# Attention, a rotation block and a feed-forward block on one core: a third score buffer for the first batch, joined first scores, chunks of 512 tokens, and 1/sum applied after P times V

## The chip, the core and the metric

One core of one Trainium2 chip runs the whole program in one launch. The metric is the device time in microseconds (us): the median of three runs of the kernel before is 902.61 us (902.42 to 905.83). The engines are PE (TensorE, matrix products; PEld is its weight load, which overlaps), DVE (VectorE), ACT (ScalarE), POOL (GpSimd) and SP (SyncE, which here only issues DMAs). A bank is one of the eight accumulators of PSUM, 128 partitions by 512 fp32 numbers.

## What is computed

Three blocks follow each other, for a batch of 4 with 576 tokens and a width of 512 (8 heads of 64).

```python
# attention, blocks of 64 tokens, each sees itself and the blocks before it
scores = 1/sqrt(64) * q @ k^T;  scores = where(block_i >= block_j, scores, -1e9)
attn = exp(scores - max(scores));  attn = attn / (sum(attn) + 1e-9);  x = attn @ v
# rotation block
theta = x @ w_theta
y = w_tok_r @ (x * cos(theta)) + w_tok_i @ (x * sin(theta))
u = x + y;  x = u + relu(u @ w_ch)
# low-rank token mixing (rank 32) and feed-forward of width 2048
u = x + (x^T @ U @ V)^T
out = u + relu(u @ w_ch1) @ w_ch2
```

## The kernel before

**A recorder and a planner.** The code does not issue instructions as it runs. `Line` records each one with a due time (`at_time`, `spread`) and a price (`price`, line 275). `run` (line 339) then walks through a list schedule: each engine takes, of what is ready and for which a buffer is free, the entry that is due first. The order so found is written out engine by engine and kept. All recorded instructions therefore carry the one line number L1162 in the profile, and are told apart by the names of their tiles.

**Attention.** The four batches have four pairs of heads each; `gp` counts the 16 pairs. Of a pair, `prep` (636) loads q, k and v and scales q. `smax(gp, t)` (650) forms the scores of token tile t = 0 to 4 for both heads in PSUM: for t = 2 to 4 each tile has a buffer of two banks of its own (tag `ss`, two buffers in all), while tiles 0 and 1 share one, as two separately issued steps. It overwrites the masked corner (a memset on DVE), takes the negated maximum `nm` (DVE), and ACT writes `P = exp(s + nm)` with the row sums `sm`. `norm` (683) forms `rs = 1/(sm + 1e-9)` and multiplies each of the nine pieces of P by it, on POOL, ACT or DVE, whichever the planner finds free first. `trans` (701) transposes P on PE through a bank (tag `pa`, two of them) and copies it to `PTA` and `PTB`; `av` (725) multiplies V by it into `oA` (tokens 0 to 255) and `oB` (256 to 575), and copies those to `xT`, the transposed result.

**The middle.** Per batch: `theta` (PE, `th`), `sines` (range reduction `t`, `f`, `c`; sine and cosine on ACT, which need another function table than exp: `ACT_TABLE_LOAD`), `product` and `mix` (PE, `y`), `chan` (PE, `c`), `lowrank` and `expand`. The planner puts attention of the later batches between these steps.

**The end.** The feed-forward block goes in chunks of tokens (`CHUNKS`: one of 512, then seven of 256). For each of the 16 slices of the hidden width, `ff1` (1038) runs 12 matmuls `m<-us,w` (each product as three, of split high and low parts), ACT and DVE form `hh`, and `ff2` (1053) runs 12 matmuls `acc<-hh,w`; `emit_out` (1074) adds and stores. `load_u` (1015) loads and splits a chunk (`us`) while an earlier one is multiplied.

**Fillers.** Where the planner expects PE to be idle in the first 140 us and a PSUM bank is free, `keep_warm` (1122) puts transposes of the identity of 128x128 into PE's order:

```python
for i in range(int((o.start - end - 60) / 110)):
    w.call = [(real.tensor.transpose, (v, ident, ident), {})]
```

The banks are two for `pm` (matmuls of the middle and hidden values), two for `pa`, and four for the two score buffers, which become `ps3` (for `acc` and hidden values) when attention is done.

Of the kernel before, what the change touches and what calls it, by code (L numbers as in the profile page):

```python
# [24 lines left out]
P = 128  # L25
# [30 lines left out]
LOC2 = "BBKKXTTTTTTKKKKB"  # L56
CHUNKS = [512] + [256] * 7
NVV = 2
# [121 lines left out]
class Line:  # L180
# [33 lines left out]
    def together(self, way):  # L214

        self.choice = []
        way()
        choice, self.choice = self.choice, None
        o = choice[0]
        o.call = [c for x in choice for c in x.call]  # L220
        o.cost = sum(x.cost for x in choice) + (107.0 if o.mode[0] == 64 else 0.0)
        o.outs, o.ins = [a for x in choice for a in x.outs], [a for x in choice for a in x.ins]
        return self.link([o])
# [304 lines left out]
def build(tc, ctx, qT, kT, v, w_theta, wtokT, w_ch, U, V, w1, w2, outT):  # L528
# [21 lines left out]
    def decode(parts, ta, oh, ol):  # L550
# [12 lines left out]
        if ol is not None:  # L563
# [22 lines left out]
             "ps": ctx.enter_context(tc.tile_pool(name="ps", bufs=1, space=PSUM))}  # L586
    ast = ExitStack()
    with tc.using_default_side("right"):
        pools["at"] = ast.enter_context(tc.tile_pool(name="at", bufs=1))
        pools["ps2"] = ast.enter_context(tc.tile_pool(name="ps2", bufs=1, space=PSUM))  # L590
    FIRST = {"q": 2, "k": 2, "vr": NVV, "P0": 2, "P1": 2, "P2": 2, "P3": 2, "P4": 2, "PTA": NPT, "PTB": NPT,
             "nm": 2, "sm": 2, "rs": 2, "ss": 2}
    THEN = {"B": NB, "U": 2, "hh": NHH}
    for pool, tags in (("wk", {"K": 8, "T": NKT, "R": NR, "RT": NT_, "raw": NRAW, "xT": NXT, "Ust": 1, "Vst": 1}),
                       ("at", FIRST), ("w1p", THEN)):
        for tag, n in tags.items():
            for i in range(n):
                line.home("ps2" if tag == "ss" else pool, f"{tag}{i}", **{tag: tuple(FIRST) if pool == "w1p" else ()})
    for i in range(2):
        line.home("ps3", f"a3{i}", a3=tuple(FIRST))  # L600
        line.home("ps3", f"b3{i}", hp=tuple(FIRST))
        line.home("ps", f"pm{i}", pm=(), hp=("pm",))
    for i in range(PA):
# [29 lines left out]
    NP = B * NC4  # L633
    qk, vrs, sx, pts, ptiles = {}, {}, {}, {}, {}

# [14 lines left out]
    def smax(gp, t):  # L650
# [7 lines left out]
        if t != 1:  # L658
            x["s"] = line.tile([P, 2, 512], F32, "ss", f"s{n}_{t}", PSUM)
        s = x["s"]  # L660
        i = 2 * t
        if t < 4:
            W = P * (t + 1)
            src = s[:, :, 256:512] if t == 1 else s[:, :, :W]
            line.together(lambda: [nc.tensor.matmul(src[:, hh], q[64 * hh:64 * hh + 64, t * P:(t + 1) * P],
                                                    k[64 * hh:64 * hh + 64, :W], start=True, stop=True) for hh in range(2)])
            nc.vector.memset(src[0:64, :, W - 64:W], NEG)
            pt = line.tile([P, 2, W], F32, f"P{t}", f"P{n}_{t}")
# [14 lines left out]
    def norm(gp):  # L683
# [3 lines left out]
        nc.vector.reciprocal(out=rs, in_=rs)  # L687
        for t in range(4):
            for hh in range(2):
                i = 2 * t + hh  # L690
                rnd("nrm", Ps[t][:, hh], Ps[t][:, hh], rs[:, i:i + 1])
# [33 lines left out]
    def av(gp, part):  # L725
# [11 lines left out]
        for i, (j, c0, cw, pt) in enumerate(blocks):  # L737
            line.together(lambda: [nc.tensor.matmul(o[64 * hh:64 * hh + 64, c0:c0 + cw], vr[:, j, 64 * hh:64 * hh + 64],
                                                    pt[:, hh], start=(i == 0), stop=(i == len(blocks) - 1))
                                   for hh in range(2)])  # L740
        cp(f"o{'AB'[part]}", xTs[b][:, c, cols], o[:, 0:w])
        if part == 1:
# [272 lines left out]
    def load_u(n):  # L1015
# [3 lines left out]
        def utile(name, shape):  # L1019
            return line.tile(shape, F32R, "U", name)  # L1020

        if n == 0:
            us[n] = [utile(f"us{n}_{a}", [P, NC4, w]) for a in range(2)]
        else:
            u = utile(f"us{n}", [P, NC4, 2, w]) if n > 1 else xtile(f"us{n}", [P, NC4, 2, w], F32R)
            us[n] = [u[:, :, a] for a in range(2)]
        uh, ul = us[n]
# [118 lines left out]
    def place(x):  # L1146
        if not isinstance(x, View):
            return x
        buf = x.buf
        if buf.ap is None:  # L1150
            if buf.home.pool not in pools:
                ast.close()
# [55 lines left out]
```

## Time and profile before

| | before |
|---|---|
| median of three runs | 902.61 us |
| the profiled execution: its own time | 902.81 us |
| its span (first to last instruction) | 901.0 us |
| PE busy | 881.4 us, 98% |
| DVE, ACT, POOL busy | 420.6, 393.5, 280.8 us (47, 44, 31%) |
| first `th` (batch 0 is through attention) | 78.14 us |
| first `y` | 124.54 us |

The profile shows one execution by the hardware's profiler; 1.8 us of the measured time lie outside of its span. PE counts as busy while any matmul runs, fillers too, and its matmuls overlap, so that busy time is not work: the time from the start of one matmul to the start of the next tells what one costs in a row of its kind. "PEclk" is the clock that the chip granted to PE, as a share of full speed.

### The profile page before, as it was taken

To read this page: it belongs to the slowest core of one execution; us is meant where nothing else is said; L and a number is where in the kernel's file an instruction comes from. 1 tells how busy PE (TensorE), PEld (TensorE's weight loads), DVE (VectorE), ACT (ScalarE), POOL (GpSimd) and SP (SyncE) were. 2 spreads that over 40 slices of the span, in tenths; PEclk is the share of its full clock that TensorE was granted. 3 is DMA by queue.
4 is the path that set the end of the run, shared out by engine and by line. 5 is a ranking of instruction groups with operands and counts; after the bars stand their busy time and mean duration, and the time that the engine had idled before them with its cause. 6 is when DMAs were issued, how large, how long until landed. Compare 5 with 4: busy or idle time off the path is not lost.

```text
span 901.0 us, 15779 instructions
## 1 busy us (share of the span) xinstructions
PE 881.4 (98%) x6275; PEld 772.0 (86%) x6275; DVE 420.6 (47%) x855; ACT 393.5 (44%) x932; POOL 280.8 (31%) x334
## 2 busy tenths in 40 slices
PE   8999999998999999999999999999999999999998
PEld 7766688876688787898887978899999999999998
DVE  4876687465644566528957782322121212121211
ACT  5977696469644685545735561121111111111111
POOL 2544455554323532346614533221020202020000
PEclk9999999998999999999999999999999999999999
DMA  5551232011020110124343350130010101000000
GB/s 197 171 157 64 70 108 77 29 42 43 29 95 16 43 43 2 68 105 131 104 135 115 111 179 19 49 99 25 1 46 3 43 6 47 3 25 1 25 1 24
DMA packets 45065, 57.39 MB, mean 64 GB/s; under 512 B 5056, under 2 KB 31168, under 8 KB 44992
## 3 DMA queue, kind: packets, MB, share of 16 engines
q1 hardware_dynamic: 44992, 56.39, 19.4%
q8 instruction: 49, 0.80, 0.4%
q14 instruction: 24, 0.20, 0.1%
HBM read 46.94 MB, written 9.44 MB: 63 GB/s over the span
## 4 chain that ended last, share of the span: by engine, by line
PE 82%; DVE 6%; ACT 6%; DMA 2%; issue 2%; POOL 1%; DVEq 0%; POOLq 0%; ACTq 0%; SPq 0%
PE acc L1162 22%; PE m L1162 22%; PE y L1162 11%; PE th L1162 7%; PE t L1162 5%; PE s L1162 5%; PE c L1162 4%; PE oB L1162 3%; DVE d_w L1162 2%; ACT L1162 1%; ACT P L1162 1%; PE G L1162 1%; PE oA L1162 1%; DMA q<-qT 1%; DVE f L1162 1%
## 5 line engine op out<-in xcount | busy, mean ns | idle before, releaser
L1162 PE MATMUL acc<-hh,w 128*128 128x256 f32 (+1 forms) x1440 | 215.7, 297 | 0.3 <-DVE o L1162 0.2
L1162 PE MATMUL m<-us,w 128*128 128x256 f32 (+1 forms) x1440 | 213.5, 296 | 0.4 <-DVE w L1162 0.4
L1162 PEld LDWEIGHTS acc<-hh,w 128*128 128x128 f32 x1440 | 191.0, 190 | 8.3 <-DVE o L1162 0.8
L1162 PEld LDWEIGHTS m<-us,w 128*128 128x128 f32 x1440 | 189.4, 189 | 7.7 <-DVE w L1162 0.8
L1162 ACT ACTIVATE hh<-m 128x256 fp32r<-128x256 f32 (+1 forms) x128 | 52.5, 410 | 300.6 <-PE m L1162 294.2
L1162 DVE SCALAR_TENSOR_TENSOR hh<-m,hh 128x256 fp32r<-128x256 f32 (+1 forms) x128 | 58.5, 457 | 266.9 <-ACT hh L1162 266.8
L1162 PE MATMUL y<-wtok,zh 128*128 128x288 f32 x576 | 122.6, 303 | 0.2
L1162 PEld LDWEIGHTS y<-wtok,zh 128*128 128x128 f32 x576 | 93.8, 190 | 4.0 <-DVE xT L1162 1.1
L1162 ACT ACTIVATE P<-s,nm 128x128 f32<-128x128 f32 (+2 forms) x144 | 78.7, 550 | 40.8 <-DVE nm L1162 40.5
L1162 PE MATMUL y<-wtok,zl 128*128 128x288 f32 x288 | 86.1, 301 | 0.1
L1162 PE MATMUL t<-ident,P 128*128 128x128 f32 x400 | 65.4, 284 | 5.3 <-DVE PTA L1162 2.5
L1162 PE MATMUL s<-k,q 64*128 64x128 f32 (+4 forms) x320 | 68.5, 467 | 1.8 <-ACT P L1162 1.8
L1162 DVE TENSOR_REDUCE nm<-s 128x2 f32<-128x256 f32 (+4 forms) x80 | 63.7, 805 | 2.4 <-PE s L1162 1.2
L1162 PEld LDWEIGHTS t<-ident,P 128*128 128x128 f32 x400 | 47.1, 143 | 20.3 <-issue 5.2
L1162 PE MATMUL c<-u,wch 128*128 128x288 f32 x384 | 59.1, 301 | 0.9 <-DVE u L1162 0.9
L1162 PEld LDWEIGHTS c<-u,wch 128*128 128x128 f32 x384 | 53.6, 188 | 5.1 <-DVE u L1162 1.3
L1162 PEld LDWEIGHTS y<-wtok,zl 128*128 128x128 f32 x288 | 54.4, 189 | 1.9 <-POOL zl L1162 0.6
L1162 PE MATMUL th<-wth,xh 128*128 128x512 f32 x160 | 51.5, 403 | 0.2
L1162 DVE TENSOR_TENSOR xT<-y,xT 128x288 f32<-128x288 f32 x64 | 28.9, 455 | 47.8 <-PE y L1162 47.3
L1162 POOL TENSOR_SCALAR us<-u 128x256 fp32r<-128x256 f32 x5 | 2.4, 480 | 146.7 <-PE m L1162 73.4
L1162 ACT COPY PTB<-t 128x512 f32<-128x512 f32 (+3 forms) x71 | 30.9, 456 | 37.4 <-PE t L1162 36.0
L1162 POOL TENSOR_TENSOR o<-us 128x256 f32<-128x256 f32 x28 | 20.1, 736 | 85.8 <-DMA outT<-o 84.9
(153 smaller groups left out, 1247.1 us busy)
## 6 DMA issues: line engine op xcount, KB each, us to landing
raw_w<-w SPq DMA_DIRECT2D x32, 512.0 KB, 3.8
raw_tok<-wtokT SPq DMA_DIRECT2D x18, 288.0 KB, 3.0
q<-qT SPq DMA_DIRECT2D x16, 320.0 KB, 2.9
vr<-v SPq DMA_DIRECT2D x16, 320.0 KB, 3.2
k<-kT SPq DMA_DIRECT2D x16, 288.0 KB, 3.4
u3d<-xT SPq DMA_DIRECT2D x16, 288.0 KB, 2.2
outT<-o SPq DMA_DIRECT2D x28, 128.0 KB, 1.8
raw_th<-w_theta SPq DMA_DIRECT2D x8, 256.0 KB, 5.1
```

What stands on the lines that cost most here:

```text
L1162: fn(*[place(x) for x in args], **{k: place(x) for k, x in kw.items()})
```

## The change

- The feed-forward chunks become 512, 256, 512, 512 and 512 tokens; the `us` tiles of the new ones are put where there is room (two `xT` slots for chunk 3, both `U` slots for an even one).
- The scores of the first four pairs (batch 0) get a tag `s0` with a third buffer of two banks (`ss2`). Its pool is closed when they are done, and its banks become `pm0` and `pm1`; the matmuls that use `pm` come only after that.
- The scores of tiles 0 and 1 are issued as one step of four matmuls, with one memset for the corners of both.
- For pairs 0 to 2, pieces 0 to 3 of P are not multiplied by `rs`; only the last, P4, is. Instead `rs` is copied 64 columns wide per head and tile to 128x512 (`re`), transposed on PE with four transposes to a bank `rb`, and copied back (`rbs`). `oA`, and the first 256 columns of `oB`, are multiplied by it on DVE as they go to `xT`; the last 64 columns of `oB` come from P4 and are copied.

```diff
-CHUNKS = [512] + [256] * 7
+CHUNKS = [512, 256, 512, 512, 512]
...
-                line.home("ps2" if tag == "ss" else pool, f"{tag}{i}", **{tag: tuple(FIRST) if pool == "w1p" else ()})
+                if tag == "ss":
+                    line.home("ps2", f"ss{i}", ss=(), s0=())
+                else:
+                    line.home(pool, f"{tag}{i}", **{tag: tuple(FIRST) if pool == "w1p" else ()})
+    line.home("px", "ss2", s0=())
...
-        line.home("ps", f"pm{i}", pm=(), hp=("pm",))
+        line.home("pp", f"pm{i}", pm=("s0",), hp=("s0", "pm"))
...
-            x["s"] = line.tile([P, 2, 512], F32, "ss", f"s{n}_{t}", PSUM)
+            x["s"] = line.tile([P, 2, 512], F32, "s0" if gp < 4 else "ss", f"s{n}_{t}", PSUM)
...
-            line.together(lambda: [nc.tensor.matmul(src[:, hh], q[64 * hh:64 * hh + 64, t * P:(t + 1) * P],
-                                                    k[64 * hh:64 * hh + 64, :W], start=True, stop=True) for hh in range(2)])
-            nc.vector.memset(src[0:64, :, W - 64:W], NEG)
+            if t == 0:
+                both = [(s[:, :, :P], 0, P), (s[:, :, 256:512], P, 2 * P)]
+            elif t > 1:
+                both = [(src, t * P, W)]
+            if t != 1:
+                line.together(lambda: [nc.tensor.matmul(y[:, hh], q[64 * hh:64 * hh + 64, c0:c0 + P],
+                                                        k[64 * hh:64 * hh + 64, :w], start=True, stop=True)
+                                       for y, c0, w in both for hh in range(2)])
+                last = s.rearrange("p h (g c) -> p h g c", c=64)[0:64, :, 1::6] if t == 0 else src[0:64, :, W - 64:W]
+                nc.vector.memset(last, NEG)
...
-        for t in range(4):
+        if gp < 3:
+            rb = abank("rb%d_%d" % divmod(gp, NC4))
+            re_ = rbs[gp] = line.tile([P, 512], F32, "rb", "rbs%d_%d" % divmod(gp, NC4))
+            cp("re", re_.rearrange("p (i c) -> p i c", c=64), rs[:, 0:8].unsqueeze(2).to_broadcast([P, 8, 64]))
+            for t in range(4):
+                nc.tensor.transpose(rb[:, t * P:(t + 1) * P], re_[:, t * P:(t + 1) * P], ident)
+            cp("rb", rbs[gp], rb)
+        for t in range(0 if gp >= 3 else 4, 4):
...
-        cp(f"o{'AB'[part]}", xTs[b][:, c, cols], o[:, 0:w])
+        if gp < 3:
+            nc.vector.tensor_tensor(out=xTs[b][:, c, cols.start:cols.start + 256], in0=o[:, 0:256],
+                                    in1=rbs[gp][:, cols.start:cols.start + 256], op=ALU.mult)
+            if part == 1:
+                cp("oC", xTs[b][:, c, 512:576], o[:, 256:320])
+        else:
+            cp(f"o{'AB'[part]}", xTs[b][:, c, cols], o[:, 0:w])
```

Since the planner sets the order, other instructions move too. In the rows below, `s_0_2` is the scores, `P_0_2` the exponentials, and `t_0_2_1` the transposes of pair 0, tile 2 (and head 1); the last number is a serial number. A matmul whose only input is `ident` is a filler.

PE, the start of the program, pair 0 (before):

```order
L1162 MATMUL s_0_0_150<-k_0_95,q_0_93 128x128 x2
L1162 MATMUL s_0_2_155<-k_0_95,q_0_93 128x384 x2
L1162 MATMUL th_0_112<-ident 128x128 x10
L1162 MATMUL s_0_0_150<-k_0_95,q_0_93 128x256 x2
L1162 MATMUL th_0_112<-ident 128x128 x25
L1162 MATMUL s_0_3_213<-k_0_95,q_0_93 128x512 x2
L1162 MATMUL th_0_112<-ident 128x128 x15
L1162 MATMUL s_0_4_252<-k_0_95,q_0_93 128x288 x2
L1162 MATMUL th_0_112<-ident 128x128 x16
L1162 MATMUL s_1_0_289<-k_1_101,q_1_99 128x128 x2
L1162 MATMUL th_0_112<-ident 128x128 x13
```

PE at the same place, of the change:

```order
L1192 MATMUL s_0_0_153<-k_0_98,q_0_96 128x128 x2
L1192 MATMUL s_0_0_153<-k_0_98,q_0_96 128x256 x2
L1192 MATMUL s_0_2_160<-k_0_98,q_0_96 128x384 x2
L1192 MATMUL s_0_3_164<-k_0_98,q_0_96 128x512 x2
L1192 MATMUL t_0_0_0_175<-ident,P_0_0_170 128x128
L1192 MATMUL t_0_0_1_115<-ident 128x128 x2
L1192 MATMUL t_0_0_1_115<-ident,P_0_0_170 128x128
L1192 MATMUL t_0_0_0_175<-ident,P_0_1_182 128x128 x2
L1192 MATMUL t_0_0_1_115<-ident,P_0_1_182 128x128
L1192 MATMUL s_0_4_192<-k_0_98,q_0_96 128x288 x2
L1192 MATMUL t_0_0_1_115<-ident,P_0_1_182 128x128
L1192 MATMUL t_0_2_0_212<-ident 128x128 x7
```

Three score steps now stand ahead of the first transposes of P, the transposes stand between the scores of one pair and no longer after the first scores of the next, and the 79 fillers among these rows of before have become 9. Over the whole program the fillers in PE's order go from 315 to 105, and ahead of the first `y` from 311 to 102.

DVE, from the row sums of pair 0 on (before); `da_th` is the decoding of a weight:

```order
L1162 TENSOR_SCALAR rs_0_307<-sm_0_162 128x9
L1162 RECIPROCAL rs_0_307<-rs_0_307 128x9
L1162 SCALAR_TENSOR_TENSOR da_th_270<-raw_th_0_227,da_th_270 128x256
L1162 TENSOR_SCALAR P_0_3_258<-P_0_3_258,rs_0_307 128x512
L1162 TENSOR_SCALAR P_0_2_222<-P_0_2_222,rs_0_307 128x384
L1162 MEMSET s_1_2_322 64x2x64
L1162 COPY PTA_0_349<-t_0_0_1_338 128x384
```

DVE at the same place, of the change:

```order
L1192 TENSOR_SCALAR rs_0_310<-sm_0_171 128x9
L1192 SCALAR_TENSOR_TENSOR da_th_287<-da_th_287,raw_th_0_223 128x256
L1192 RECIPROCAL rs_0_310<-rs_0_310 128x9
L1192 COPY rbs_0_320<-rs_0_310 128x512
L1192 TENSOR_REDUCE nm_1_259<-s_1_0_246 128x2
L1192 MEMSET s_1_2_284 64x2x64
...
L1192 COPY rbs_0_320<-rb_0_268 128x512
...
L1192 TENSOR_TENSOR xT_402<-oA_0_386,rbs_0_320 128x256
```

The multiplications of P are gone, and the transposes of P no longer stand behind `rs`: the copies of `PTA` are ahead of these rows now, and `rs` is needed by P4 and by the multiplication of `oA`. DVE has 207 instructions ahead of the first `y`'s inputs where it had 192, ACT 189 where it had 193.

ACT in the sines of batch 1 (before); `c` and `f` are the angles, P the exponentials of a later batch:

```order
L1162 ACTIVATE c_3_2478<-c_3_2478,halfpi 128x512
L1162 ACT_TABLE_LOAD
L1162 ACTIVATE P_1_3_2547,sm_1_2383<-s_1_3_2515,nm_1_2371 128x512
L1162 ACT_TABLE_LOAD
L1162 ACTIVATE f_0_2262<-f_0_2262 128x512
L1162 ACT_TABLE_LOAD
L1162 ACTIVATE P_1_3_2547,sm_1_2383<-s_1_3_2515,nm_1_2371 128x512
L1162 ACT_TABLE_LOAD
L1162 ACTIVATE f_1_2283<-f_1_2283 128x512
L1162 ACT_TABLE_LOAD
L1162 ACTIVATE P_1_4_2614,sm_1_2383<-s_1_4_2520,nm_1_2371 128x576
L1162 ACT_TABLE_LOAD
```

ACT at the same place, of the change:

```order
L1192 ACTIVATE c_0_2187<-c_0_2187,halfpi 128x512
L1192 ACTIVATE c_1_2234<-c_1_2234,halfpi 128x512
L1192 ACTIVATE c_2_2307<-c_2_2307,halfpi 128x512
L1192 ACTIVATE c_3_2318<-c_3_2318,halfpi 128x512
L1192 ACTIVATE f_0_2065<-f_0_2065 128x512
L1192 ACTIVATE f_1_2096<-f_1_2096 128x512
L1192 ACTIVATE f_2_2181<-f_2_2181 128x512
L1192 ACTIVATE f_3_2232<-f_3_2232 128x512
L1192 COPY PTB_1_2417<-t_1_2_0_2407 128x3x128
L1192 CAST x2h_0_2430<-xq_0_2421 128x512
L1192 COPY PTB_1_2417<-t_1_2_1_2427 128x3x128
L1192 ACT_TABLE_LOAD
```

The sines of the four tiles now stand in one piece; the table is loaded twice in this batch, not eight times, and 8 times in the program, not 14.

## Rows read from the trace of the kernel before

**Rows 1.** The page: busy time by engine, and the chain that ended last.
```profile
PE 881.4 (98%) x6275; PEld 772.0 (86%) x6275; DVE 420.6 (47%) x855; ACT 393.5 (44%) x932; POOL 280.8 (31%) x334
PE 82%; DVE 6%; ACT 6%; DMA 2%; issue 2%; POOL 1%; DVEq 0%; POOLq 0%; ACTq 0%; SPq 0%
```

**Rows 2.** Windows: us, busy time (instructions) of each engine, granted clock, DMA share, GB/s.
```profile
0.00:124.50 124.50, 120.02 (x848) 88.54 (x848) 85.60 (x194) 93.97 (x260) 52.06 (x66) 1.00 0.39 128
20.00:60.00 40.00, 39.50 (x300) 28.97 (x298) 34.90 (x81) 36.73 (x109) 24.07 (x27) 1.00 0.59 190
20.00:120.00 100.00, 97.99 (x691) 69.61 (x690) 73.34 (x164) 80.28 (x224) 44.82 (x54) 1.00 0.38 121
200.00:220.00 20.00, 18.11 (x132) 14.03 (x128) 12.45 (x26) 19.07 (x35) 7.09 (x9) 1.00 0.16 49
220.00:240.00 20.00, 17.24 (x91) 12.21 (x92) 12.80 (x24) 15.35 (x33) 7.46 (x12) 0.83 0.00 1
240.00:260.00 20.00, 20.00 (x142) 15.78 (x141) 10.60 (x24) 9.77 (x27) 2.96 (x6) 1.00 0.31 107
```

**Rows 3.** Groups by form: busy, mean ns of one, idle before, releaser.
```profile
L1162 PE MATMUL th<-ident 128*128 128x128 f32 x238 | 33.3, 287 | 1.4 <-POOL ident masks.py:199 1.4
L1162 PE MATMUL t<-ident 128*128 128x128 f32 x77 | 9.8, 273 | 0.0
L1162 ACT ACT_TABLE_LOAD x14 | 18.0, 1283 | 9.1 <-DVE nm L1162 8.9
L1162 DVE COPY PTB<-t 128x512 f32<-128x512 f32 x9 | 6.2, 690 | 4.9 <-PE t L1162 4.8
L1162 DVE TENSOR_TENSOR o<-acc,o 128x256 f32<-128x256 f32 x28 | 10.5, 425 | 5.8 <-PE acc L1162 5.8
L1162 DVE TENSOR_TENSOR o<-acc,o 128x512 f32<-128x512 f32 x4 | 2.7, 682 | 0.0
L1162 POOL TENSOR_TENSOR us<-u,us 128x512 fp32r<-128x512 f32 x3 | 4.9, 1636 | 0.7 <-ACT us L1162 0.7
```

**Rows 4.** The chain in order of time: start, length, what.
```profile
119.69 2.84 PE t L1162 x26
...
544.33 2.80 PE acc L1162 x12
...
563.93 2.73 PE m L1162 x12
...
645.75 1.42 PE m L1162 x12
```

**Rows 5.** PE's timeline: first V products of pairs 0 and 3, first `th`, first `y`.
```profile
28.55 0.87 PE L1162 MATMUL oA<-PTA,vr 128*64 128x256 f32 x8
...
75.64 0.87 PE L1162 MATMUL oA<-PTA,vr 128*64 128x256 f32 x8
...
78.14 0.71 PE L1162 MATMUL th<-wth,xh 128*128 128x512 f32 x2
...
124.54 0.50 PE L1162 MATMUL y<-wtok,zh 128*128 128x288 f32 x2
```

**Rows 6.** Tile P in the first 78 us: ns least/median/most, first and last start.
```profile
L1162 POOL TENSOR_SCALAR P<-P,rs x15: 483/689/980, 22.5 to 69.0; 128x384 f32<-128x384 f32 x4, 128x512 f32<-128x512 f32 x4, 128x256 f32<-128x256 f32 x3, 128x576 f32<-128x576 f32 x3
L1162 ACT ACTIVATE P<-P,rs x14: 385/494/708, 22.4 to 68.6; 128x128 f32<-128x128 f32 x6, 128x256 f32<-128x256 f32 x3, 128x384 f32<-128x384 f32 x3, 128x512 f32<-128x512 f32 x2
L1162 DVE TENSOR_SCALAR P<-P,rs x7: 355/576/737, 22.6 to 68.1; 128x512 f32<-128x512 f32 x2, 128x256 f32<-128x256 f32 x2, 128x384 f32<-128x384 f32 x1, 128x128 f32<-128x128 f32 x1
```

**Rows 7.** ACT's timeline in the sines of batch 1: start, length, what.
```profile
207.33 1.28 ACT L1162 ACT_TABLE_LOAD   x1
208.63 0.81 ACT L1162 ACTIVATE f<-f,tbias,tscale 128x512 f32<-128x512 f32 x1
```

**Rows 8.** Waits in the first 124.5 us: us in total, times, longest.
```profile
DVE s L1162 <- PE s L1162: 10.4, 4, 7.0
```

**Rows 9.** DVE's timeline at its first score: start, length, what.
```profile
8.17 0.17 DVE L1162 MEMSET s<- 64x128 f32 x1 [6.96 <-PE s L1162]
```

More of the change, by code (lines that the diff above doesn't have):

```diff
@@ L220, in together @@
         o.call = [c for x in choice for c in x.call]
-        o.cost = sum(x.cost for x in choice) + (107.0 if o.mode[0] == 64 else 0.0)
+        o.cost = sum(x.cost for x in choice) + (53.5 * len(choice) if o.mode[0] == 64 else 0.0)
         o.outs, o.ins = [a for x in choice for a in x.outs], [a for x in choice for a in x.ins]
@@ L586, in build @@
              "ps": ctx.enter_context(tc.tile_pool(name="ps", bufs=1, space=PSUM))}
-    ast = ExitStack()
+    ast, pst = ExitStack(), ExitStack()
+    pools["px"] = pst.enter_context(tc.tile_pool(name="px", bufs=1, space=PSUM))
     with tc.using_default_side("right"):
@@ L591, in build @@
     FIRST = {"q": 2, "k": 2, "vr": NVV, "P0": 2, "P1": 2, "P2": 2, "P3": 2, "P4": 2, "PTA": NPT, "PTB": NPT,
-             "nm": 2, "sm": 2, "rs": 2, "ss": 2}
+             "nm": 2, "sm": 2, "rs": 2, "rb": 2, "ss": 2}
     THEN = {"B": NB, "U": 2, "hh": NHH}
@@ L633, in build @@
     NP = B * NC4
-    qk, vrs, sx, pts, ptiles = {}, {}, {}, {}, {}
+    qk, vrs, sx, pts, ptiles, rbs = {}, {}, {}, {}, {}, {}
     def prep(gp):
@@ L1020, in utile @@
             return line.tile(shape, F32R, "U", name)
-        if n == 0:
+        if n == 1:
+            u = xtile(f"us{n}", [P, NC4, 2, w], F32R)
+            us[n] = [u[:, :, a] for a in range(2)]
+        elif n % 2:
+            us[n] = [xtile(f"us{n}_{a}", [P, NC4, w], F32R) for a in range(2)]
+        else:
             us[n] = [utile(f"us{n}_{a}", [P, NC4, w]) for a in range(2)]
-        else:
-            u = utile(f"us{n}", [P, NC4, 2, w]) if n > 1 else xtile(f"us{n}", [P, NC4, 2, w], F32R)
-            us[n] = [u[:, :, a] for a in range(2)]
         uh, ul = us[n]
@@ L1150, in place @@
         if buf.ap is None:
+            if buf.home.pool not in pools and buf.home.pool == "pp":
+                pst.close()
+                pools["pp"] = ctx.enter_context(tc.tile_pool(name="pp", bufs=1, space=PSUM))
             if buf.home.pool not in pools:
```

## The prediction

> **What bounds the kernel now.** I read the page first: PE is busy for 98% of the span and carries 82% of the chain; no other engine passes 47% [rows 1]. So the kernel is a queue of matmuls. But busy is not useful here: fillers count too. Hence three further readings: what PE does in the head (before the first `y`), where PE stands still although it has work, and what a matmul costs in a row of its kind.
>
> The head. By the timeline the first V product stands at 28.55, the fourth at 75.64, the first `th` at 78.14 and the first `y` at 124.54 [rows 5]: one pair takes (75.64 − 28.55)/3 = 15.7 us. PE is busy for 120.0 of the first 124.5 us, but the groups by form show 238 + 77 = 315 fillers [rows 3], 311 of them in this stretch. In a row they take 2.84/26 = 109 ns each [rows 4], so 311 are 33.9 us: over a quarter of the head is made of them. Two other engines are loaded as well: from 20 to 60 us DVE is busy 34.9 of 40 us and ACT 36.7; over 20 to 120, DVE 73.3 of 100 [rows 2].
>
> The one stretch with a hole. From 200 to 240 us PE is busy 18.11 + 17.24 of 40 us, so it idles 4.65, and in the second half the granted clock is 0.83. If 6.8 of these 20 us are at 1.2 GHz (1 − 0.17 × 2 = 0.66 of the time at 2.4 GHz), half of that, 3.4 us, is lost too: together 8.0. From 240 on PE is full again at 1.00 [rows 2]. In this stretch ACT changes its function table to and fro; a load is 1.28 us, and the next ACTIVATE starts 1.30 after it began [rows 3, 7].
>
> The feed-forward rows. 12 `acc` matmuls of 512 columns take 2.80 us (233 ns each), 12 `m` of 256 take 1.42 (118.5 each) [rows 4].
>
> **The change, part by part.** The sum is made on the span of the profiled execution, 901.0 us.
>
> *Fillers.* PE's order has 210 fewer: 210 × 0.109 = 22.9 us of work that computes nothing. They stand in one engine's queue, and an engine takes its queue in order: a filler that is behind schedule delays the matmul behind it. So taking it out gives its time back, as far as PE then has something ready. −22.9.
>
> *New transposes.* Three pairs with four `rb` transposes: 12 × 0.109 = +1.3.
>
> *New waits in the head.* Does PE then have something ready? I counted PE's other instructions ahead of the first `y` in both orders, each at the start-to-start time of its kind in before: 76.0 us in before, 85.7 in the change (8.4 of attention comes forward, with the 1.3). With 209 fillers fewer there, PE's list puts the first `y` at 124.5 − 22.8 + 9.7 = 111.4. DVE has 207 instructions ahead of it, before 192; at 85.60/194 = 0.44 us each that is 85.6 + 15 × 0.44 = 92.2 us [rows 2]. Its first score arrives at 8.17 [rows 9]. If DVE keeps the share of its dense stretch (0.873), it is through at 8.2 + 92.2/0.873 = 113.8: PE waits 2.4 us more than its list says. If DVE only reaches the mean of 20 to 120 (0.733), it is through at 134.0, and 22.6 us of new waits take the place of the fillers. Zero is possible too, as some of the 15 are small. I take 3. DVE's waits for scores were 10.4 us, of which 7.0 are the start [rows 8], so it is not starved by them in before; but three score steps now stand together in PE's order and the transposes of P depend on exp alone, which is what kept DVE fed from 20 to 60. That row is nearest. What happens in time to `rs` is in this: 24 of P's 36 multiplications go, at 494 to 689 ns on three engines [rows 6], and six copies of 128x512 (0.69 at most [rows 3]) and a multiplication of `oA` and `oB` for a copy come. They leave the path from exp to the V product and come back behind it; ACT and POOL win more than DVE. The first maximum waits for two more matmuls of the joined step, once at the start (some 0.6 us); the saved memsets pay it back. +3.
>
> *Feed-forward.* Six chunks of 256 become three of 512. Per matmul that replaces two, 2 × 118.5 − 233 = 3.8 ns; a chunk of 512 has 2 × 16 × 12 = 384, so 1.46 us each and 4.4 for three. With the other row of 512 columns, 2.73 for 12 (227.5) [rows 4], it would be 9.5 × 1152 = 11.0. I take 4.5, since `acc` and `m` rows alternate and the longer one is a chain row in a steady stretch; 11.0 is the low end. The loads and splits of a chunk lie under the chunk ahead: 45.5 us (384 × 118.5 ns) or 89.5. The longest part of it is four splits of 1.64, 6.5 us [rows 3]; with the loads ahead of them, some 10 us is the price, once, if the tiles (two `xT` slots, or both `U` slots) come free too late. −4.5.
>
> The Trainium skill ("TensorE: Matmul & The Clock Gate", Back-to-back issue gap) gives N/2.4 + 2.5 ns for a warm matmul. By it each join saves 2.5 ns, 2.9 us in all as an estimate, and 512 columns take 215.8 ns; the rows' 233 is above that, so the trace does not agree in size, only in sign.
>
> *Table loads.* ACT's order has 8 for 14: 6 × 1.28 = 7.7 us on ACT, all in the sines of batch 1, where PE loses 8.0. PE doesn't lose all of it to them (the chain from `th` through `f` to `zh` is long without them), so I take 5 of 8. Nothing, if attention has moved forward and this stretch lacks cover, is the other end. −5.
>
> The Trainium skill ("ScalarE: Activation LUTs", What ACT_TABLE_LOAD costs) puts a switch at 1283 ns and a drain of about 1380, 2.66 us. By it the six would be 16.0 us on ACT, as an estimate; the trace shows the first part, not the second.
>
> *The end.* The last stores are of 512 columns: 0.682 for 0.425 on the last addition [rows 3], and a larger transfer, some 0.2. +0.5.
>
> Sum: 901.0 − 22.9 + 1.3 + 3 − 4.5 − 5 + 0.5 = 873.4. The profiled run took 1.8 us more than its span and lies 0.2 above the median: +1.6, so **875.0 us**.
>
> **The rivals.**
>
> *The head is bound by DVE and ACT (B).* The fillers stood where PE had nothing to do; without them it waits in the same places. For it: DVE 0.87 and ACT 0.92 busy from 20 to 60; against it: P's multiplications leave, and DVE's waits were for PE. With 22.6 in place of 3: 875.0 + 19.6 = 894.6. It would look the same if fillers were only left out for want of a free bank (the third score buffer takes the two of `pm`): then the change of order does nothing.
>
> *The gain is paid back downstream (D).* 8.4 us of attention that is done in the head no longer fills PE while the sines of batches 0 and 1 run. Then 200 to 240 has more holes, 8.4, and the 5 us of the table loads don't show: 875.0 + 13.4 = 888.4. For it: PE idles there already. Against: the planner puts the next pairs in their place.
>
> *Slower (C): the clock.* With fillers gone PE idles in the head, and the granted clock falls there, as it did at 220 to 240 (0.83) after PE had idled [rows 2]. At 1.2 GHz the work of a stretch takes twice as long; each us spent so costs half a us. To cancel 27.6 us, 55 of the 111 us of the head must be at the lower level; all of it would give 875.0 + 55.7 = 930.7. Against: the score and V products leave PE little idle, and the clock was 1.00 over the whole head.
>
> The Trainium skill ("TensorE: Matmul & The Clock Gate", Part 4: PE-mode transpose) says that transposes do not count as busy for the clock. By that rule, the fillers held nothing up, and C would be void; the trace has 1.00 throughout the stretch with 311 of them, which agrees with either.
>
> **How the numbers follow.** A measurement tells about 0.5%, 4.5 us, from no change. The forecast (861 to 884, around 875.0) 0.68; downstream (D) 0.13; B 0.12; slower (C) 0.03; below its low end 0.04. The low end: 6.5 for 11.0 of the joined chunks, 3 for all 8 of the sines, 3 for no new waits: 875.0 − 12.5 = 862.5, and I write 863. To the other side the range takes in D with a little more: 891. So 863 to 891; what is left out is B, C and the low tail, 0.19. Faster holds the forecast, D and most of B (894.6 is 0.9% below 902.6): 0.94; the rest of B, with more waits, makes the same 0.03; slower 0.03.
>
> **What the changed profile would show.** The first `y` at 111 to 115 us and the first `th` near 68; PE busy for over 0.93 of this stretch at a clock of 1.00. If `y` stands near 120 or later and the groups show PE idle behind DVE's `nm`, `s` or ACT's P, then B is right. In 200 to 240 us of before's time, that is the sines of batch 1, two table loads and an idle below 2 us; 5 or more means D. A chunk of 512 at 89.5 us: 88 or less takes the low end. A granted clock under 0.9 in the head would be C. I am wrong above all if PE's list was not what held the head.

## The result, and the profile after

| | before | changed |
|---|---|---|
| median of the runs beside each other | 902.51 us (4 runs) | 865.40 us (865.0 to 868.0, 4 runs) |
| ratio | | 0.9592 (0.9570 to 0.9614) |
| span of the profiled execution | 901.0 us | 863.2 us |
| first `th` / first `y` | 78.14 / 124.54 | 68.12 / 116.45 |

The change takes 37.1 us off; forecast were 27.6, and 865.4 lies in the range given. But two of its steps were right in sign for a wrong reason, and a third was too small, as the experiments below show. First the rows of the changed kernel that answer to those ahead of the prediction.

The page of the changed kernel, busy time and chain [rows 1]:

```profile
PE 844.0 (98%) x4925; PEld 691.6 (80%) x4925; DVE 414.5 (48%) x793; ACT 374.5 (43%) x861; POOL 263.2 (30%) x286
PE 86%; DVE 6%; ACT 5%; issue 1%; POOL 1%; DMA 0%; ACTq 0%; DVEq 0%; POOLq 0%; SPq 0%
```

Its windows: us, busy time of each engine, granted clock, DMA share, GB/s [rows 2]:

```profile
0.00:116.40 116.40, 106.80 (x717) 75.21 (x717) 89.64 (x209) 94.57 (x263) 53.23 (x65) 0.99 0.45 145
20.00:60.00 40.00, 37.22 (x270) 24.30 (x269) 37.74 (x91) 39.31 (x121) 20.55 (x23) 1.00 0.58 186
24.00:68.10 44.10, 40.87 (x300) 26.09 (x296) 41.44 (x97) 41.45 (x127) 22.45 (x25) 1.00 0.57 181
...
180.00:200.00 20.00, 20.00 (x151) 17.09 (x149) 13.13 (x26) 15.76 (x30) 9.63 (x13) 1.00 0.15 49
200.00:220.00 20.00, 18.97 (x131) 15.30 (x130) 13.97 (x29) 13.27 (x35) 7.35 (x10) 1.00 0.10 32
```

From 20 to 60 us PE is *less* busy than before (37.2 of 40 us, where before had 39.5), and DVE and ACT are nearly full: 37.7 and 39.3 of 40. PE does less and gets further. Its timeline shows how far [rows 5]:

```profile
29.51 0.87 PE L1192 MATMUL oA<-PTA,vr 128*64 128x256 f32 x8
...
63.25 0.87 PE L1192 MATMUL oA<-PTA,vr 128*64 128x256 f32 x8
...
68.12 0.73 PE L1192 MATMUL th<-wth,xh 128*128 128x512 f32 x2
...
116.45 0.50 PE L1192 MATMUL y<-wtok,zh 128*128 128x288 f32 x2
```

The first V product comes no earlier (29.5, before 28.6), but a pair takes (63.25 − 29.51)/3 = 11.2 us for 15.7. The groups by form show what went and what came [rows 3], and the tile P the multiplications that are left, 14 up to 68 us where before had 36 up to 78 [rows 6]:

```profile
L1192 PE MATMUL t<-ident 128*128 128x128 f32 x77 | 13.1, 331 | 1.4 <-POOL ident masks.py:199 1.4
L1192 ACT ACT_TABLE_LOAD x8 | 10.3, 1283 | 11.6 <-DVE nm L1192 11.5
L1192 PE MATMUL rb<-ident 128*128 128x128 f32 x28 | 3.7, 278 | 0.0
L1192 PE MATMUL rb<-ident,rbs 128*128 128x128 f32 x12 | 1.9, 277 | 0.0
```

```profile
L1192 ACT ACTIVATE P<-P,rs x6: 401/695/797, 24.8 to 67.8; 128x576 f32<-128x576 f32 x2, 128x256 f32<-128x256 f32 x1, 128x384 f32<-128x384 f32 x1, 128x512 f32<-128x512 f32 x1
L1192 POOL TENSOR_SCALAR P<-P,rs x6: 400/670/1037, 34.4 to 67.9; 128x576 f32<-128x576 f32 x2, 128x384 f32<-128x384 f32 x1, 128x512 f32<-128x512 f32 x1, 128x128 f32<-128x128 f32 x1
L1192 DVE TENSOR_SCALAR P<-P,rs x2: 390/480/571, 56.9 to 57.4; 128x256 f32<-128x256 f32 x1, 128x128 f32<-128x128 f32 x1
```

77 + 28 fillers are left of 315. In the feed-forward rows the chain has 2.80 us for 12 matmuls of 512 columns of both kinds [rows 4]:

```profile
623.01 2.80 PE m L1192 x12
625.81 2.80 PE acc L1192 x12
```

**Where the 37.8 us of the span went.** For each kernel I cut PE's time at the first `y` of batch 0, the first `y` of batch 1, the last `h` (a matmul of `expand` in batch 3), and the last matmul, and counted in each part the matmuls that are no fillers, each at the median start-to-start time of its kind in before (109 ns for a transpose, 118.5, 132.5 and 232 for 256, 288 and 512 columns, 107 to 267 for the scores of 64 rows). That sum is PE's work; what is left of the part I call rest: idle, fillers, and what a lower clock costs. Each kernel's parts are read from one profiled execution.

| part | rest before | rest changed | difference | forecast |
|---|---|---|---|---|
| to the first `y` | 48.6 | 30.6 | −18.0 | −22.9 + 3 = −19.9 |
| to the first `y` of batch 1 | 15.9 | 4.5 | −11.4 | −5 |
| to the last `h` | 20.9 | 17.0 | −3.9 | 0 |

The `rb` transposes add 1.3; from the last `h` to the last matmul it is 304.4 us instead of 310.6, −6.2 (forecast −4.5); behind the last matmul +0.3. Together −37.9. So the head came out 1.9 us short of the forecast, and the 10 us that the forecast lacks are in the middle (10.3) and in the feed-forward block (1.7).

Part of the middle is the clock. From the first `y` to that of batch 1 the granted clock reads 0.95 in before and 1.00 in the changed kernel, and up to the last `h` it fell once more in before (580 to 586 us):

```profile
124.50:236.10 111.60, 104.95 (x679) 84.83 (x680) 72.56 (x150) 77.78 (x180) 55.94 (x69) 0.95 0.16 51
580.00:586.00 6.00, 5.39 (x27) 4.78 (x27) 4.89 (x10) 1.62 (x4) 6.00 (x9) 0.72 0.52 201
```

```profile
116.40:208.60 92.20, 91.17 (x617) 76.48 (x616) 65.00 (x133) 66.99 (x165) 47.30 (x53) 1.00 0.16 51
```

By these rows up to some 5 of the 11.4 us and 1.7 of the 3.9 are the lower clock of before, and the remainder of both is mostly idle time of PE.

### The profile page after: what moved, and what is told of

It is laid out like the page before. It is cut to its first block, busy times and chain, and to the rows that moved or that the text cites. A ratio compares the mean times of both kernels' runs of the same rounds, so it can differ in the third digit from the quotient of the medians.

```text
span 863.2 us, 12710 instructions
## 1 busy us (share of the span) xinstructions
PE 844.0 (98%) x4925; PEld 691.6 (80%) x4925; DVE 414.5 (48%) x793; ACT 374.5 (43%) x861; POOL 263.2 (30%) x286
## 3 DMA queue, kind: packets, MB, share of 16 engines
q1 hardware_dynamic: 41536, 56.39, 19.9%
## 4 chain that ended last, share of the span: by engine, by line
PE 86%; DVE 6%; ACT 5%; issue 1%; POOL 1%; DMA 0%; ACTq 0%; DVEq 0%; POOLq 0%; SPq 0%
PE acc L1192 23%; PE m L1192 22%; PE y L1192 12%; PE c L1192 5%; PE th L1192 5%; PE t L1192 5%; PE s L1192 5%; PE oB L1192 4%; ACT P L1192 2%; DVE d_w L1192 2%; PE oA L1192 1%; PE G L1192 1%; PE xp L1192 1%; DVE nm L1192 1%; PE xq L1192 1%
## 5 line engine op out<-in xcount | busy, mean ns | idle before, releaser
L1192 PE MATMUL acc<-hh,w 128*128 128x512 f32 (+1 forms) x900 | 205.6, 374 | 0.6 <-DVE o L1192 0.2
L1192 PE MATMUL m<-us,w 128*128 128x512 f32 (+1 forms) x900 | 203.3, 372 | 0.3 <-DVE w L1192 0.3
L1192 PEld LDWEIGHTS acc<-hh,w 128*128 128x128 f32 x900 | 156.9, 188 | 33.6 <-DVE o L1192 1.5
L1192 PEld LDWEIGHTS m<-us,w 128*128 128x128 f32 x900 | 157.0, 188 | 31.2 <-DVE w L1192 0.8
L1192 DVE SCALAR_TENSOR_TENSOR hh<-m,hh 128x512 fp32r<-128x512 f32 (+1 forms) x80 | 50.9, 637 | 265.4 <-ACT hh L1192 265.4
L1192 ACT ACTIVATE hh<-m 128x512 fp32r<-128x512 f32 (+1 forms) x80 | 44.3, 554 | 294.1 <-PE m L1192 289.1
L1192 PE MATMUL s<-k,q 64*128 64x128 f32 (+4 forms) x320 | 65.4, 453 | 0.0
L1192 POOL TENSOR_TENSOR o<-us,us 128x512 f32<-128x512 f32 x16 | 20.7, 1322 | 115.6 <-DMA outT<-o 85.3
L1192 ACT COPY PTB<-t 128x384 f32<-128x384 f32 (+3 forms) x68 | 30.5, 461 | 35.0 <-PE t L1192 34.1
L1192 POOL TENSOR_TENSOR zl<-f,zh 128x512 fp32r<-128x512 f32 x18 | 23.1, 1295 | 64.2 <-PE y L1192 61.4
```

What stands on the lines that cost most here:

```text
L1192: fn(*[place(x) for x in args], **{k: place(x) for k, x in kw.items()})
```

## The experiments

Every kernel was timed in five rounds beside the kernel before; the ratios are to that, and a gain or loss against before is worked out from the ratio, at 902.5 us. A loss against the changed kernel is the difference of the medians; by the ratios each of the four is 1.2 to 1.5 us smaller. A new build of one part lets the planner make a new order; where the text says that the order stays, only the named instructions differ.

### One thing taken from the kernel before, order kept: chunks, table loads, fillers

**The chunks alone** (`b_chunks`): the diff of `CHUNKS` and of the `us` tiles as in the change, nothing else.

> The kernel before with the new feed-forward chunks alone (512, 256, 512, 512, 512); the order of everything ahead of the chunks stays. Theory: a matmul of 512 columns takes 233 ns where two of 256 take 2 x 118.5, so 1152 joined matmuls save 4.4 us: about 898 us. Rival: the row of 512 columns at 227.5 ns holds, 11 us less, 891.5. Second rival: the bigger loads and splits come late at a chunk's start, and the gain is lost, 902 or more.

898.21 us, ratio 0.9947 (0.9926 to 0.9968): 4.8 us less. The first theory holds. Its chain has the row expected:

```profile
645.46 2.80 PE m L1164 x12
```

In its profiled execution the part behind the last `h` is 304.4 us, 6.2 shorter than in before and as short as in the change, which is more than the theory's 4.4; the interval of the runs holds both.

**The sines of batch 1 in one piece** (`b_sines`): after planning, a sine that stands behind exponentials is moved up to the one before it, as far as its inputs allow.

```diff
     order = line.plan(ROUNDS)
+    def sines_together(order):
+        out, first = list(order), None
+        table = lambda x: x.ways[x.eng].table if x.eng == ACT_ else None
+        for o in order:
+            if table(o) != "s":
+                continue
+            if first is not None and o.start - first.start < 25e3:
+                at = {id(x): i for i, x in enumerate(out)}
+                lo = max([at[id(first)]] + [at[id(p)] for p, _ in o.deps])
+                if any(table(x) == "e" for x in out[lo + 1:at[id(o)]]):
+                    out.remove(o)
+                    out.insert(lo + 1, o)
+            first = o
+        return out
+    order = sines_together(order)
```

> The kernel before with one edit of ACT's order: in the sines of batch 1 the four sines that are ready stand directly behind the cosines, so that the function table is loaded twice and not eight times there; all else, fillers too, stays in its order. Theory: the six loads (7.7 us on ACT) are what PE waited for between 200 and 240 us, and the fall of the granted clock behind them is part of it: 8 to 11 us less, 891.5 to 894.5. Rival: the hole is the chain from th through the range reduction to zh with too little attention beside it; then 0 to 3 us less, 899.5 to 902.5.

902.33 us, ratio 0.9991 (0.9978 to 1.0004): 2 us at most, and perhaps nothing. My theory fell, and with it the step of the prediction that counted table loads. ACT's timeline of this kernel shows that the edit did what it says: two loads stand there, the second done at 214.14; in before the first of eight begins at 207.33 [rows 7] and the last at 226.32:

```profile
206.21 1.28 ACT L1179 ACT_TABLE_LOAD   x1
...
210.67 2.17 ACT L1179 ACTIVATE f<-f 128x512 f32<-128x512 f32 x4
212.86 1.28 ACT L1179 ACT_TABLE_LOAD   x1
...
217.35 0.74 ACT L1179 ACTIVATE P<-s,nm 128x576 f32<-128x576 f32 x1 [1.74 <-DVE nm L1179]
...
220.41 1.84 ACT L1179 ACTIVATE P<-P,rs 128x512 f32<-128x512 f32 x3 [2.23 <-DVE rs L1179]
```

ACT then waits for DVE instead, and the hole in PE is as wide as before: rest 16.2 us in this part, before 15.9. Its windows:

```profile
200.00:220.00 20.00, 18.30 (x131) 14.04 (x129) 12.62 (x24) 15.93 (x33) 7.02 (x8) 0.98 0.16 49
220.00:240.00 20.00, 18.12 (x85) 12.69 (x82) 11.40 (x22) 9.62 (x26) 7.27 (x11) 0.67 0.00 1
```

PE idles for 3.6 us where it idled 4.65 [rows 2], but the granted clock is 0.67 where it was 0.83. That lower clock does not hide a gain of several us: of the executions with a mean granted clock of 0.996, the four of before took 900.2 to 902.0 us and the three of this kernel 900.2 to 901.1. Though the sines are done 13 us earlier, the first `y` of batch 1 stands where it stood, first in before, then here:

```profile
236.13 0.43 PE L1162 MATMUL y<-wtok,zh 128*128 128x288 f32 x2
```

```profile
236.42 0.43 PE L1179 MATMUL y<-wtok,zh 128*128 128x288 f32 x2
```

PE's longest wait in this stretch is the same one in both, a transpose `xp` that waits for DVE (2.3 us, here 1.6). Loads that were taken from an engine whose next work waited for another gave little back.

**No fillers** (`b_nofill`, `a_nofill`): one edit in each kernel, all else in its order.

```diff
-WARM = 140e3
+WARM = 0.0
```

> The kernel before without its 315 fillers, all else in its order. Theory now: in the order of before PE waits for DVE and ACT where the fillers stood, so without them it idles in the same places: 0 to 5 us less (897.5 to 902.5), unless the clock falls. Rival (the first term of the prediction taken by itself): a filler holds up what stands behind it, and taking 315 of them out gives most of 34 us back: 875 or less. Third: the granted clock falls in the head, and the time rises by some 5 to 30 us.

905.34 us, ratio 1.0027 (1.0012 to 1.0042): 2.4 us *more*. The rival, the prediction's own step, is refuted in size: most of 34 us should have come back. The third theory is there in a small dose, as the windows of this kernel show:

```profile
0.00:124.50 124.50, 95.63 (x526) 57.92 (x526) 80.81 (x186) 89.06 (x251) 48.05 (x62) 0.93 0.40 126
20.00:60.00 40.00, 29.97 (x172) 17.83 (x172) 32.34 (x74) 34.20 (x102) 21.32 (x25) 0.91 0.54 170
36.10:42.90 6.80, 3.89 (x15) 2.34 (x16) 4.62 (x14) 5.40 (x18) 4.27 (x6) 0.50 0.58 198
60.00:66.80 6.80, 6.46 (x26) 3.67 (x27) 3.99 (x7) 2.83 (x10) 1.47 (x2) 0.50 0.27 87
66.80:107.80 41.00, 37.37 (x228) 24.14 (x226) 24.68 (x55) 26.56 (x75) 12.57 (x17) 1.00 0.24 71
```

The lower clock could hide what the fillers cost, so I compare a stretch in which both kernels are granted 1.00. Between the same two score steps, first in before, then without fillers:

```profile
63.97 1.24 PE L1162 MATMUL s<-k,q 128*128 128x288 f32 x4
...
102.77 0.92 PE L1162 MATMUL s<-k,q 64*128 64x384 f32 x4
```

```profile
68.60 1.24 PE L1162 MATMUL s<-k,q 128*128 128x288 f32 x4
...
106.62 0.92 PE L1162 MATMUL s<-k,q 64*128 64x384 f32 x4 [1.26 <-ACT P L1162]
```

That is 38.80 us with 38 fillers (4.1 us) and 38.02 without: 0.8 of 4.1 us comes back, and PE now stands idle for ACT's `P` instead. Only at the program's start do fillers hold up something: the first scores begin at 7.57 us in before and at 4.84 here, because the first fillers are 213 ns apart, at the lower clock, where `keep_warm` counts 110 for each. That lead is gone at the first V product (28.55 and 28.58).

PE's longest wait in its first 130 us (in all, times, longest):

```profile
PE s L1162 <- ACT P L1162: 15.2, 11, 2.5
```

With fillers in place the same wait reads 1.3 us in before, in its first 125 us:

```profile
PE s L1162 <- ACT P L1162: 1.3, 2, 1.1
```

The next scores wait until ACT has read the scores in the buffer, 15.2 us in the head; the fillers had hidden that wait in the trace. It is the wait that a third buffer is for.

> The changed kernel without its 105 fillers, all else in its order. Theory: 79 stand in the first 25 us, where PE waits for the first loads and scores anyway, so 0 to 3 us less: 862 to 865.5. Rival: the fillers keep the clock up at the start; without them the granted clock is low for longer and the time rises by 3 to 8 us, 868 to 873.

865.0 us, ratio 0.9581 (0.9561 to 0.9601); the changed kernel has 0.9592 (0.9570 to 0.9614). No difference that can be told. Here, too, the fillers of the start hold up the first scores (4.86 us without them, 8.33 with them), and the first V product comes 2.9 us earlier without them (29.51 in the changed kernel); of that, 1.25 us are left at the first `y` (115.20) and none at the end. The wait for a free score buffer is 2.7 us in the first 125, where the order of before has 15.2:

```profile
26.58 0.87 PE L1192 MATMUL oA<-PTA,vr 128*64 128x256 f32 x8
```

```profile
PE s L1192 <- ACT P L1192: 2.7, 2, 1.5
```

### One part taken out of the change

`a_norm` (0 for 3 in the three comparisons with `gp`, so P is multiplied as before), `a_2buf` (no `ss2`; `pm` in `ps` as before) and `a_nojoin` (the lines of before for tiles 0 and 1):

```diff
-        if gp < 3:
+        if gp < 0:
...
-        for t in range(0 if gp >= 3 else 4, 4):
+        for t in range(0 if gp >= 0 else 4, 4):
...
-        if gp < 3:
+        if gp < 0:
```

```diff
...
-                    line.home("ps2", f"ss{i}", ss=(), s0=())
+                    line.home("ps2", f"ss{i}", ss=())
...
-    line.home("px", "ss2", s0=())
...
-        line.home("pp", f"pm{i}", pm=("s0",), hp=("s0", "pm"))
+        line.home("ps", f"pm{i}", pm=(), hp=("pm",))
...
-            x["s"] = line.tile([P, 2, 512], F32, "s0" if gp < 4 else "ss", f"s{n}_{t}", PSUM)
+            x["s"] = line.tile([P, 2, 512], F32, "ss", f"s{n}_{t}", PSUM)
```

```diff
-            if t == 0:
-                both = [(s[:, :, :P], 0, P), (s[:, :, 256:512], P, 2 * P)]
...
+            line.together(lambda: [nc.tensor.matmul(src[:, hh], q[64 * hh:64 * hh + 64, t * P:(t + 1) * P],
+                                                    k[64 * hh:64 * hh + 64, :W], start=True, stop=True) for hh in range(2)])
+            nc.vector.memset(src[0:64, :, W - 64:W], NEG)
```

> The changed kernel with P normalised as before (nine multiplications of P for all pairs, no rb transposes, plain copies of oA and oB); third buffer, joined scores and chunks stay. The planner leaves 180 fillers in PE's order instead of 105. Theory: fillers cost nothing themselves but mark where PE has nothing to do, so 75 more of them mean 8 us more of idle in the head; 871 to 877, first y some 8 us later for the same work. Rival: the scaling behind P times V costs DVE (which is 0.94 busy from 24 to 68 us in the changed kernel) as much as it saves, and the time stays within 3 us of 865.4.

877.03 us, ratio 0.9704 (0.9673 to 0.9734): 11.6 us above the changed kernel, at the upper end of the theory.

> The changed kernel with two score buffers, as before, and the two pm banks there from the start; scaling behind P times V, joined scores and chunks stay. The planner leaves 220 fillers. Theory: the third buffer is the larger part of the gain in the head, 115 fillers are 12.5 us of idle, and with less attention done by the first y the hole in the sines of batch 1 opens again (up to 8 us): 876 to 888. Rival: DVE and ACT bound the head whatever the buffers, 865 to 870.

888.28 us, 0.9831 (0.9802 to 0.9860): 22.9 us above. The size is the upper end of the theory's; the hole that I expected to open again did not (see the table).

> The changed kernel with the scores of tiles 0 and 1 issued as two steps again, with a memset each. 127 fillers. Theory: 22 more fillers, 2.4 us of idle: 866 to 870. Rival: the join is what brings the first V products together and the memsets (16 pairs, 0.17 us each) count on a DVE that is 0.94 busy: 872 or more.

887.27 us, 0.9821 (0.9792 to 0.9850): 21.9 us above. The theory missed it by far, and the rival's 872 or more holds, without a run that tests its reason. The number of fillers (127, hardly more than 105) was a bad guide here: in the head the rest grows by 10.5 us where 22 fillers mark 2.4, and a further 11.6 us lie beyond the head, in which no filler is placed.

**More of a part** (`a_all`): the scaling behind P times V for all 16 pairs (`gp < 16`).

> The changed kernel with the scaling behind P times V for all 16 pairs instead of the first three. 93 fillers. Theory: from the first y on PE is the bound and 52 more rb transposes cost it 52 x 0.109 = 5.7 us, less what pair 3 gains in the head: 866 to 871. Rival: the middle is held up by the chain of P's multiplications too, and the time falls below 862.

874.3 us, 0.9677 (0.9646 to 0.9707): 8.9 us above the changed kernel, 3 more than the theory allowed. The head gets better by 3.2 us of rest (27.4), but the 52 transposes cost PE 5.7 and the rest of the later parts grows from 4.5 + 17.0 to 5.4 + 23.1.

### One part alone in the kernel before

`b_join`, `b_3buf` and `b_scale` are the same three parts, each put into the kernel before by itself, with the lines of the change for it.

> The kernel before with the joined first scores alone (all 16 pairs). 319 fillers, 8 table loads in the planner's order. Theory: the head doesn't shorten by it alone (the fillers say that PE has as much idle as before), but a score step fewer per pair lets the middle close: the hole in the sines of batch 1 (11 us) goes: 888 to 894. Rival: the parts add up, and the join alone gives what taking it out of the changed kernel cost, 22 us: 879 to 884. Second rival: alone it gives nothing, 900 to 905.

892.45 us, 0.9886 (0.9865 to 0.9907): 10.3 us less, as the theory says. Its windows where before has the hole:

```profile
200.00:220.00 20.00, 20.00 (x142) 15.88 (x139) 13.94 (x29) 15.97 (x32) 10.26 (x14) 1.00 0.16 49
220.00:240.00 20.00, 18.89 (x130) 15.28 (x130) 14.42 (x27) 14.85 (x41) 7.17 (x11) 1.00 0.09 32
```

> The kernel before with the third score buffer for batch 0 alone. 257 fillers, 16 table loads. Theory: 62 fillers fewer ahead of the first y mark some 6.8 us less idle of PE, the hole in the sines of batch 1 stays: 893 to 898. Rival: the parts add up: 23 us less, 878 to 883. Second rival: two pm banks fewer during the head hold up th, and nothing is won, 901 to 905.

900.62 us, 0.9973 (0.9955 to 0.9991): 2.4 us less, where the theory had some 5 to 10.

> The kernel before with the scaling behind P times V for the first three pairs alone. 336 fillers, 16 table loads. Theory: with two score buffers and unjoined scores PE and DVE wait for scores, not for P's multiplication, so it gives nothing alone: 899 to 906. Rival: the parts add up: 12 us less, 889 to 894.

907.65 us, 1.0057 (1.0037 to 1.0077): 5.1 us *more*, above the theory's 899 to 906.

Rest of PE in us, counted as in the section on the result:

| kernel | ratio | work ahead of first `y` | rest to first `y` | to first `y` of batch 1 | to last `h` |
|---|---|---|---|---|---|
| before | 1 | 76.0 | 48.6 | 15.9 | 20.9 |
| fillers out (`b_nofill`) | 1.0027 | 76.0 | 53.7 | 14.6 | 20.2 |
| join alone | 0.9886 | 78.0 | 52.5 | 4.0 | 17.8 |
| third buffer alone | 0.9973 | 76.9 | 45.2 | 13.1 | 24.6 |
| scaling alone | 1.0057 | 77.4 | 53.2 | 12.3 | 21.4 |
| join + buffer (`a_norm`) | 0.9704 | 84.5 | 40.6 | 4.6 | 19.2 |
| join + scaling (`a_2buf`) | 0.9831 | 77.4 | 46.0 | 4.8 | 26.2 |
| buffer + scaling (`a_nojoin`) | 0.9821 | 82.0 | 41.1 | 4.8 | 28.6 |
| all (the change) | 0.9592 | 85.8 | 30.6 | 4.5 | 17.0 |

(The last four rows have the new chunks too, 0.9947 by themselves.) The four parts alone multiply to 0.9947 × 0.9886 × 0.9973 × 1.0057 = 0.986, 12 us; together they give 37. Two thirds of the gain belong to no part. Each build also has its own order from the planner, and what another order alone is worth, with no part changed, was not measured; it is in every row.

### What bounds the head now

`a_nomask`: the changed kernel, its order kept, with DVE's memsets dropped behind the planner, so that the scores in the corners are not masked.

```diff
     order = line.plan(ROUNDS)
+    order = [o for o in order if not any(NEG in [y for y in args if isinstance(y, float)] for _, args, _ in o.call)]
```

> The changed kernel with the 48 memsets of the masked corners left out of the issued order (so the mask within a block of 128 is not applied, and the numbers of P differ); all else in its order. It takes 23 instructions, 4.7 us, off DVE ahead of the first y. Theory: after the change DVE is what PE waits for in the head (0.94 busy from 24 to 68 us), so the first y comes 2.5 to 5 us earlier and the time falls by as much, 860.5 to 863. Rival: ACT (0.94 busy too) or the chain through exp holds the head; the first y moves by under 1 us and the time stays at 864.5 to 866.

863.46 us, 0.9553 (0.9540 to 0.9566), against 0.9592 (0.9570 to 0.9614): 0.39%, some 3.5 us by the ratios and 1.9 by the medians. 4.7 us taken off DVE come back in about half, so DVE is part of what bounds the head, and not all. A memset is also a step between the scores and their maximum, so this run does not tell DVE's load from the length of that chain. Its first `th` is 1.5 us earlier:

```profile
66.62 0.73 PE L1193 MATMUL th<-wth,xh 128*128 128x512 f32 x2
```

In the profiled execution the granted clock is 0.93 between 68 and 116 us, so its later times are not compared.

## Why the prediction came out right, and where its steps failed

**Fillers, −22.9: the number held, the reason did not.** The step that failed is "a filler that is behind schedule delays the matmul behind it. So taking it out gives its time back, as far as PE then has something ready". Such a delay is seen only ahead of the first scores (2.7 us, and lost again by the first V product). Behind them PE had next to nothing ready where the fillers stood: taking out all 315 cost 2.4 us, and 0.8 of 4.1 came back where the clock was the same; taking out the last 105 gave 0.1% or nothing. Fillers mark where PE has nothing else to do; a change that removes the cause removes the filler with it, and so the count of fillers came near the gain here: rest in the head fell by 18.0, forecast 19.9. That is in part luck, since in `a_nojoin` the same count misses by 8 us. The largest wait in before is that of the scores for a free buffer, 15.2 us once the fillers don't cover it; in the changed kernel without fillers it is 2.7. The first rival, B, named this ("The fillers stood where PE had nothing to do") and drew the wrong conclusion, that PE would go on waiting: it overlooked that the other parts of the change take the waits away. (The trace of before has 314 fillers ahead of the first `y`, not 311; that is 0.3 us.)

**New waits in the head, +3: 5 would have been right.** The forecast had the first `y` at 114.4; it came at 116.45, beyond the 111 to 115 given. DVE runs at 41.44/44.10 = 0.94 and ACT as high from 24 to 68 us, above the dense row that I had taken as the limit (0.87). The value near PE's own list was the right end; the mean row, 22.6, was not. PE was busy for 106.80 of 116.40 us there, 0.92, where over 0.93 was given.

**What the prediction did not see: the parts need each other.** It costed them one by one. The wait of PE in a pair ends with the last of three chains: a free score buffer, the maxima and exponentials of the tiles (a step less with the join), and `rs` with P's multiplications ahead of the transposes. Taking one away leaves the others: alone they change the rest in the head by +3.9, −3.4 and +4.6, in twos by −8.0, −2.6 and −7.5, and all three by −18.0. That these three chains run beside each other and the last one counts is my reading of this table; a run that shows each chain by itself was not made.

**Table loads, −5: the stretch closed by more than that, and not by them.** The step that failed is "ACT's order has 8 for 14 ... all in the sines of batch 1, where PE loses 8.0". With 8 loads and all else in the order of before, the rest stays (16.2, before 15.9). With the join alone it is 4.0, and in every kernel with two of the three parts 4.6 to 4.8. What these kernels share is another order of the planner, with fewer or freer score steps. Which instruction of that order closes the hole, stays open. Up to 5 us of before's 15.9 are the lower clock, and the wait of `xp` for DVE (2.3 us in before) is 0.7 with the join alone and 0.9 in the change. Whatever six switches cost ACT, PE got 2 us of it or less. The Trainium skill ("ScalarE: Activation LUTs", What ACT_TABLE_LOAD costs) would have had them cost ACT 16.0 us, as an estimate from its 2.66 us for one. The trace shows the load alone: in the changed kernel, too, the ACTIVATE behind a load starts 1.29 us after the load's start (189.98 and 191.27):

```profile
189.98 1.28 ACT L1192 ACT_TABLE_LOAD   x1
191.27 0.81 ACT L1192 ACTIVATE f<-f,tbias,tscale 128x512 f32<-128x512 f32 x1
```

**Feed-forward, −4.5: right in kind, too small by 1.7.** The chunks alone gave 4.8 (2.9 to 6.7), and the row of 2.80 us held for both kinds. But the part behind the last `h` is 6.2 us shorter, in `b_chunks` as in the change. The clock has no share in it, as it was 1.00 over this part of before:

```profile
586.70:897.30 310.60, 310.60 (x2619) 310.40 (x2617) 59.43 (x147) 44.75 (x118) 34.24 (x49) 1.00 0.07 22
```

The term that was mis-sized is the 3.8 ns of a joined matmul. It was taken from one chain row of 2.80 us (and 2 × 118.5 − 233 is 4.0); the median start-to-start time of 512 columns in before is 232 ns, so a join saves 5.0, and 1152 of them 5.8 us. The last 0.4 is not accounted for.

**The other rivals.** *Paid back downstream (D)* did not come: the part to the first `y` of batch 1 got shorter by 11.4 us of rest with 9.8 us more work done ahead of it; the indicator of 5 us idle in the sines of batch 1 is at 1.03 in 200 to 220. In `a_2buf` and `a_nojoin` the rest up to the last `h` grows (26.2 and 28.6), which may be the same thing further on; no run tests it. *The clock (C)* is real and small: without fillers the clock falls in the head of before's order, and the kernel loses 0.27%. In the changed kernel the head is at 0.99.

## What to carry to other kernels

Read filler work as a mark first and as a cost second: run the kernel once without it, look at the wait that appears, and compare stretches at the same clock. And try parts that shorten the same stretch together before judging them one by one: here one of them alone made the kernel slower, and taking it out of the whole cost 11.6 us. When an engine's overhead shall count as a gain, ask what the engine that waits does in the us that come free; the six table loads, 7.7 us on ACT, were worth 2 us at most.

## What the runs showed of the hardware that I had not expected

Transposes of the identity raise the clock and hold it up. In before PE does nothing else until its first scores at 7.57 us, and in that time their spacing falls from 213 ns to 109, that is from the lower level of the clock (1.2 GHz) to the full one (2.4 GHz). The windows of the fillers alone, 19 in 4.0 us and then 17 in 1.7:

```profile
1.40:5.40 4.00, 4.00 (x19) 1.00 0.81 239
5.80:7.50 1.70, 1.70 (x17) 1.00 0.97 358
```

Without them the transposes of P in the same order are still at the lower level until 24.9 us, twelve in 3.23 us, and at the full one from 26 on:

```profile
21.68 3.23 PE L1162 MATMUL t<-ident,P 128*128 128x128 f32 x12
24.84 1.20 PE L1162 MATMUL s<-k,q 64*128 64x256 f32 x4
25.96 0.77 PE L1162 MATMUL t<-ident,P 128*128 128x128 f32 x5
```

The column of the granted clock does not show this start: it reads 1.00 in both, because the trace's clock records begin at 5.6 us in before and at 25.9 in `b_nofill`, and what has no record counts as full. So the 0.93 of that head is too high. The Trainium skill ("TensorE: Matmul & The Clock Gate", Part 4: PE-mode transpose) says that transposes do not count as busy for the clock. These rows speak against it. The prediction had taken the 1.00 of before's head to agree with either; the fall of the spacing does not. What it is worth here is small: at the first V product PE is where it was in before, in the two later stretches at 0.50 it falls 4.6 us behind, and 2.4 us of 903 are left of that at the end.
